# Other places in the step order for weight maxima, second-layer weight work, conversions and low parts, and another order of the last blocks' parts

## The chip, the cores and the metric

One core of one Trainium2 chip runs the kernel. The time is that of one execution on the device in microseconds; shorter is better. The kernel before takes 1488.77 us, the median of three runs between 1488.62 and 1488.83.

## The reference

Two parts follow one another: a gated linear attention over 4 batches, 8 heads, 768 positions and 48 columns a head, and a layer of 8 experts over the 3072 tokens that come out of it. The routing weights P are balanced in eight rounds, and every expert computes every token.

```python
f = 1.0 / (1.0 + np.exp(-f_logit))
for t in range(S):
    state = f[:, :, t, :, None] * state + np.einsum('bhd,bhe->bhde', k[:, :, t], v[:, :, t])
    y[:, :, t] = np.einsum('bhd,bhde->bhe', q[:, :, t], state)
...
logits = x @ w_gate                      # x: (3072, 384), 8 experts
P = np.exp(logits - logits.max())
for _ in range(8):
    P /= P.sum(1, keepdims=True) + 1e-09
    P /= P.sum(0, keepdims=True) + 1e-09
    P *= N / E
for e in range(E):
    h = np.maximum(x @ w1[e], 0.0)       # w1[e]: (384, 1024)
    out += P[:, e:e + 1] * (h @ w2[e])   # w2[e]: (1024, 384)
```

## The kernel before

Engine names are those of the profile: PE multiplies matrices, PEld loads its weights, DVE is the vector engine, ACT the scalar engine, POOL the general one, SP issues transfers.

**Numbers.** An fp32 operand of a product is split into two fp16 tensors, a high part (name with h: w1h, xh, hh, kh) written by ACT as a scaled copy, and a low part (w1l, xl, hl, kl) written by DVE or POOL as operand minus high part. A product is then three PE products: high by high, high by low, low by high.

**First part, up to about 491 us.** The attention runs in chunks (`early_item` for the first three items, `item` for the others; tiles q, kb, ql, vl, am, u, st, sl, aps, kvps, xl). As soon as a block of tokens has its output, experts 0 and 1 compute it in the plain way (`moe_tile`, `moe`): first layer into the bank hps, hh and hl from it, second layer into the bank yps, copied by ACT to yr and written to DRAM. These products fill PE between the attention's. The weights of the two experts come from `load`: SP starts the transfer into w1r or w2r, ACT makes w1h or w2h, DVE makes w1l or w2l, each at a step of its own. Which step is written out by hand: `FIRSTAT` and `SECONDAT` give, for each of the eight pieces of expert 0 and of expert 1, the steps at which its ACT and its DVE instruction are issued; `FILL` says how many products of the plain experts are put into a step. Instructions of an engine run in the order in which they are issued (`pin` chains them), so a step number is a place in every engine's queue. The Sinkhorn rounds and the conversion of the tokens for the second part (`convert`: sums xs by POOL, xah and xbh by ACT, xal and xbl by DVE, three maxima xmx a batch by DVE) follow, started at the steps `CONVSTEP` and `KSTEP`.

**Second part, from about 491 us.** Experts 2 to 7 are computed with fewer products. There are 48 periods (6 experts, 2 halves of the hidden columns, 4 batches; the table `ORDER`). A period multiplies tokens by first-layer weights as 3x3 blocks by 3x2 blocks in 15 block products (`PRODUCTS`); 15 linear forms of the tokens (xa, xb) and of the weights (k1h, k1l) go in, and the products are added up in the PSUM banks A to F. `SLOTS` gives the order of the 15 products with their banks; after each product comes what `EVENTS` lists for it: ACT copies a bank (cp), DVE adds a copy to a bank or starts bank E or F from bank D and a copy (init), ACT and DVE read the finished blocks (kh, kl, kah, kal, and the sums kr and kf), and ACT and DVE or POOL split the sums (kgh, kgl). Between the products of a period stand those of the second layer of the period before: three blocks (`paired`), each of which goes through eight parts with seven block products into the banks kyps and kxps, whose sums (part, xx, yy, acc) ACT, DVE and POOL form. A bank that is read has to be left before PE writes it again: this is how PE comes to wait for DVE and ACT.

Other work is given to a product's number by further tables: `W1AT` (`W1AT0` in period 0) for a piece of first-layer weights (`prepare_w1`: transfer k1r, sums k1s by POOL, a maximum wmx, k1h by ACT, k1l by DVE), `W2AT` (`W2AT0`, `W2AT1`, `W2AT3` in the first periods) for a piece of second-layer weights (`prepare_w2`: k2r, wmx, k2h, sums k2s, k2l), `READDAT` for the outputs of experts 0 and 1 that come back from DRAM (`readds`: yb, scaled by ACT to yz, added to acc by POOL), `MAXAT` for the maxima of the weights of experts 0 and 1 (`first_maxima`: a transfer k1rm or k2rm, then a maximum wmx), `CHECKAT` for other checks, `CONVAT` for the conversion of the last batch. The maxima feed a test at the end (`verdict`, tiles gd_t, gd_r, flag) of whether the fp16 scales suited the data.

After period 47 the blocks not yet finished are carried on by the string `ENDING`, one character a step: a dot issues the events of the next product number, a digit takes two parts of that block, v one step of the test. `ENDX` names the banks of these blocks.

Of the kernel before, what the change touches and what calls it, by code (L numbers as in the profile page):

```python
# [19 lines left out]
C = 64  # L20
# [4 lines left out]
KT = 3  # L25
# [62 lines left out]
ENDING = '.0.11.0.1..12.v12.22....vv32v3v34v3vvvvv4v34vv44'
# [188 lines left out]
def fast(ctx, tc, qkf, vbd, wg, w1, w2, out, flag):  # L277
# [83 lines left out]
    def load(e, k, j):  # L361
# [13 lines left out]
        ws[e][k - 1].append(pair)  # L375
# [13 lines left out]
    def moe(e, u, w):  # L389
# [5 lines left out]
        for f in range(FT):  # L395
# [4 lines left out]
            for a, x, k in [(wh, x, k) for k in range(KT) for x in (xh, xl)] + [(wl, xh, k) for k in range(KT)]:  # L400
                mm(out=ps, lhsT=a[:, k, fs], rhs=x[:, k, :], start=(n == 0), stop=(n == 8))
                n += 1
                if n < 9:
                    yield 1
# [1085 lines left out]
```

## Time and profile before

| | |
|---|---|
| median of three runs | 1488.77 us |
| the profiled execution's own time | 1490.45 us |
| its span, first to last instruction | 1488.7 us |
| mean granted clock of PE | 0.995 |
| busy: PE, PEld | 98%, 85% |
| busy: DVE, ACT, POOL | 86%, 70%, 70% |
| moved by DMA | 96.01 MB |
| PE's longest single wait (start, for DVE's ind) | 3.0 us |

A row of the timeline reads: start in the span, duration, engine, line, operation, result and operands, number of instructions, and in brackets the idle time ahead of it with the instruction that ended it. Names have no buffer numbers there, so that kb_A stands for bank A of every period. PE's products run one into the other: a product of 256 columns is shown with about 0.27 us and begins some 0.11 us after the one ahead of it, so a wait shorter than about 0.16 us does not appear in the brackets. A row of the stretches reads: from and to, length, and then the busy time of PE, PEld, DVE, ACT and POOL, each with its number of instructions, PE's granted clock (1.00 is full), the share of the DMA engines and GB/s.

### The profile page before, as it was taken

How to read it: one execution, taken by the hardware profiler on the slowest of the kernel's cores; microseconds unless marked ns; L12 is line 12 of the kernel's file. 1: busy time of each engine (PE TensorE's matmuls, PEld its weight loads, DVE VectorE, ACT ScalarE, POOL GpSimd, SP SyncE). 2: the span in 40 equal slices, each digit the busy share in tenths (PEclk: the TensorE clock that was granted, in tenths of full speed). 3: DMA queues.
4: the chain of work that ended last, by engine and by line, in shares of the span. 5: the costliest groups of instructions: out<-in, count | busy, mean ns of one | idle time of the engine just before them, and what ended most of it. 6: DMA issues, size and time to landing. Idle time of an engine off the chain costs nothing. (4 is left out here: it accounts for less than half of the span.)

```text
span 1488.7 us, 40252 instructions
## 1 busy us (share of the span) xinstructions
PE 1457.8 (98%) x16051; PEld 1266.0 (85%) x16051; DVE 1279.4 (86%) x2507; ACT 1035.6 (70%) x2310; POOL 1039.4 (70%) x1203
## 2 busy tenths in 40 slices
PE   7999999999999999999999999999999999999997
PEld 4788887666666789999999999999999999999996
DVE  8878988896677698999999999999999999888876
ACT  6655556554434777887887888888877777777764
POOL 2244444455427666899999998999988888888763
PEclk9999999999999999999999999999999999999999
DMA  9455645541000101221112111111110011000012
GB/s 276 122 134 135 142 118 130 142 103 50 22 33 29 52 12 29 61 61 55 47 57 65 56 56 44 52 55 55 49 33 28 28 34 33 12 13 23 2 54 78
DMA packets 82806, 96.01 MB, mean 64 GB/s; under 512 B 49872, under 2 KB 66384, under 8 KB 82608
## 3 DMA queue, kind: packets, MB, share of 16 engines
q1 hardware_dynamic: 82176, 92.75, 22.6%
q8 instruction: 127, 2.08, 0.6%
q14 instruction: 71, 0.58, 0.1%
q10 hardware_dynamic: 432, 0.59, 0.1%
HBM read 69.53 MB, written 14.16 MB: 56 GB/s over the span
## 5 line engine op out<-in xcount | busy, mean ns | idle before, releaser
L305 PEld LDWEIGHTS <-k1h 128*128 128x128 f16 x2880 | 270.4, 98 | 31.8 <-issue 7.2
L305 PE MATMUL kyps<-k2h,kgh 128*128 128x192 f16 x1152 | 283.6, 246 | 1.0 <-ACT part L1197 1.0
L305 PE MATMUL kyps<-k2l,kgh 128*128 128x192 f16 x1152 | 283.6, 246 | 0.0
L305 PE MATMUL kyps<-k2h,kgl 128*128 128x192 f16 x1152 | 283.6, 246 | 0.0
L305 PEld LDWEIGHTS <-kgh 128*128 128x128 f16 x2304 | 212.4, 98 | 7.9 <-issue 1.3
L1370 POOL TENSOR_TENSOR kgl<-kf,kgh 128x512 f16<-128x512 f32 x141 | 182.4, 1293 | 6.4 <-ACT kgh L1367 6.2
L1239 POOL TENSOR_TENSOR acc<-acc,yy 128x384 f32<-128x384 f32 x129 | 129.3, 1002 | 76.3 <-DVE yy L1200 76.2
L1370 POOL TENSOR_TENSOR kgl<-kr,kgh 128x512 f16<-128x512 f32 x141 | 172.2, 1221 | 11.2 <-ACT kgh L1367 11.2
L1200 DVE SCALAR_TENSOR_TENSOR yy<-kyps,pes,part 128x192 f32<-128x192 f32 x258 | 107.1, 415 | 73.0 <-PE kyps L305 68.1
L305 PEld LDWEIGHTS <-k1l 128*128 128x128 f16 x1440 | 141.0, 98 | 16.5
L305 PE MATMUL yps<-w2h,hl 128*128 128x384 f16 x384 | 125.9, 328 | 2.2 <-DVE hl L457 2.1
L305 PE MATMUL yps<-w2l,hh 128*128 128x384 f16 x384 | 125.9, 328 | 1.4 <-DVE w2l L377 1.4
L305 PE MATMUL yps<-w2h,hh 128*128 128x384 f16 x384 | 125.9, 328 | 0.0
L305 PEld LDWEIGHTS <-w1h 128*128 128x128 f16 x1344 | 97.2, 98 | 33.6 <-issue 2.6
L305 PEld LDWEIGHTS <-kh 128*128 128x128 f16 x1152 | 108.2, 98 | 8.9 <-issue 2.5
L305 PEld LDWEIGHTS <-kgl 128*128 128x128 f16 x1152 | 112.8, 98 | 0.2 <-issue 0.2
L305 PEld LDWEIGHTS <-hh 128*128 128x128 f16 x768 | 74.4, 98 | 45.1 <-issue 1.0
L305 PE MATMUL hps<-xl,w1h 128*128 128x128 f16 (+1 forms) x672 | 109.2, 257 | 1.3 <-DVE xl L666 0.6
L305 PE MATMUL hps<-xh,w1h 128*128 128x128 f16 (+1 forms) x672 | 109.0, 257 | 0.1
L1197 ACT ACTIVATE kyps<-kyps 128x192 f32<-128x192 f32 x144 | 46.2, 321 | 79.5 <-PE kyps L305 77.4
L1367 ACT ACTIVATE kgh<-kf 128x512 f16<-128x512 f32 x144 | 91.9, 639 | 0.6 <-DVE kf L1344 0.6
L1367 ACT ACTIVATE kgh<-kr 128x512 f16<-128x512 f32 x144 | 91.3, 634 | 0.2
(298 smaller groups left out, 5306.0 us busy)
## 6 DMA issues: line engine op xcount, KB each, us to landing
q<-in_qkf_dram SPq DMA_DIRECT2D x23, 672.0 KB, 5.0
vr<-in_vbd_dram SPq DMA_DIRECT2D x24, 384.0 KB, 3.9
k1r<-in_w_dram SPq DMA_DIRECT2D x24, 384.0 KB, 3.1
ys<-yr SPq DMA_DIRECT2D x48, 192.0 KB, 2.9
k2r<-in_w_dram SPq DMA_DIRECT2D x24, 384.0 KB, 3.1
yb<-ys SPq DMA_DIRECT2D x48, 192.0 KB, 2.8
out_dram<-acc SPq DMA_DIRECT2D x21, 192.0 KB, 1.9
w1r<-in_w_dram SPq DMA_DIRECT2D x8, 384.0 KB, 10.0
```

The source lines that it names most:

```text
L305: ins = (nc.tensor.transpose if transpose else nc.tensor.matmul)(**kw)
L1197: pin(nc.scalar.activation(out=out, in_=in_, func=AF.Copy, **kw))
L1200: pin(nc.vector.scalar_tensor_tensor(out=y, in0=ps, scalar=p, in1=z, op0=ALU.mult, op1=ALU.add))
L1239: pin(nc.gpsimd.tensor_tensor(out=y, in0=y, in1=z.rearrange("p s d -> p (s d)"), op=ALU.add))
L1367: pin(nc.scalar.activation(out=hs['g', t][0][i], in_=hs['f' if i else 'r', t], func=AF.Copy))
L1370: pin((nc.vector if tag == str(PERIODS - 1) else nc.gpsimd).tensor_tensor(out=hs['g', t][1][i], in0=hs['f' if i else 'r', t], in1=hs['g', ...
```

## The change

Both kernels have the same instructions; what differs is their order on each engine. The tables after the change, each with what stood there before:

```diff
 EVENTS: after product n the listed events
-          6: (('init', 'E', '-', 6, 'D'), ('copy', 'A', 0)), ...
-          9: (('gf', 'A', 0), ('copy', 'C', 7), ('gd', 0, 'P')),
+          5: (('init', 'E', '-', 6, 'D'),), 6: (('copy', 'A', 0),), ...
+          9: (('gd', 0, 'P'), ('gf', 'A', 0), ('copy', 'C', 7)),
...
-          21: ..., 23: (('gh', 2, 1),), 24: (('gl', 2, 1),), 26: (('gl', 2, 0),)}
+          21: ..., 23: (('gh', 2, 1),), 25: (('gl', 2, 1),), 26: (('gl', 2, 0),)}
-W2AT = (3, 22, 25, 25, 27, 29, 30, 34, 38)
+W2AT = (4, 22, 25, 25, 27, 29, 30, 35, 39)
-READDAT = (9, 13)
+READDAT = (9, 14)
-MAXAT = (1, 10)
+MAXAT = (0, 6)
-ENDX = ('x', 'k0', 'x', 'k0')
+ENDX = ('x', 'k1', 'k0', 'k0')
-ENDING = '.0.11.0.1..12.v12.22....vv32v3v34v3vvvvv4v34vv44'
+ENDING = '.0.101..1..21v..12.v22.v..3v233v434vvvvvv3v444vv'
-CONVSTEP = (25, 53, 71)
-KSTEP = 43
+CONVSTEP = (28, 55, 70)
+KSTEP = 39
...
 for the two plain experts and the attention:
-            for a, x, k in [(wh, x, k) for k in range(KT) for x in (xh, xl)] + [(wl, xh, k) for k in range(KT)]:
+            for a, x in ((wh, xh), (wl, xh), (wh, xl)):
+                for k in range(KT):
...
-                for m, (a, x) in enumerate(((0, vh), (0, vl), (1, vh))):
+                for m, (a, x) in enumerate(((0, vh), (1, vh), (0, vl))):
...
-            for m, (a, x) in enumerate(((kh, qh), (kh, ql), (kl, qh))):
+            for m, (a, x) in enumerate(((kh, qh), (kl, qh), (kh, ql))):
```

`FIRSTAT`, `SECONDAT`, `W1AT0`, `W2AT0`, `W2AT1`, `W2AT3` and `CONVAT` have other numbers too, mostly by one to three steps, in `CONVAT` by up to thirteen; `load` puts its pair at a fixed index instead of appending it; three entries are added to `FILL` and a name for the batches that POOL converts, with the values that applied before. In the lines of the second kernel all numbers are one or two higher.

What this moves on DVE is seen in three places. The first is at 52 to 58 us of the profile before: carry is the attention's state, w1l_2 and w1l_3 are weights of the second expert, xl the low part of the attention's output (in these rows names stand without the expert's number and with a buffer number at the end). Before:

```order
L377 SCALAR_TENSOR_TENSOR w1l_0_869<-w1r_0_496,w1h_0_868 128x768
L377 SCALAR_TENSOR_TENSOR w1l_1_872<-w1r_1_537,w1h_1_871 128x768
L588 TENSOR_TENSOR carry_1001<-kvps_1_974,st_831 112x384
L377 SCALAR_TENSOR_TENSOR w1l_2_895<-w1r_2_556,w1h_2_894 128x768
L377 SCALAR_TENSOR_TENSOR w1l_3_898<-w1r_3_578,w1h_3_897 128x768
L666 SCALAR_TENSOR_TENSOR xl_301<-yps_925,xh_300 96x3x128
L666 SCALAR_TENSOR_TENSOR xl_301<-yps_925,xh_300 32x128 x3
```

After:

```order
L378 SCALAR_TENSOR_TENSOR w1l_2_895<-w1r_2_556,w1h_2_894 128x768
L378 SCALAR_TENSOR_TENSOR w1l_0_869<-w1r_0_497,w1h_0_868 128x768
L378 SCALAR_TENSOR_TENSOR w1l_1_872<-w1r_1_538,w1h_1_871 128x768
L590 TENSOR_TENSOR carry_1002<-kvps_1_972,st_831 112x384
L668 SCALAR_TENSOR_TENSOR xl_301<-yps_923,xh_300 96x3x128
L668 SCALAR_TENSOR_TENSOR xl_301<-yps_923,xh_300 32x128 x3
L378 SCALAR_TENSOR_TENSOR w1l_3_995<-w1r_3_578,w1h_3_994 128x768
```

Of the two w1l between carry and xl, w1l_3 has gone behind xl and w1l_2 ahead of w1l_0 and carry.

The second place is at 64 to 71 us: wmx<-k2r is the maximum over a piece of second-layer weights of the second part, the two hl are the low parts for one tile of the second expert, ql and vl belong to the attention. Before:

```order
L377 SCALAR_TENSOR_TENSOR w2l_3_1105<-w2r_3_706,w2h_3_1104 128x768
L718 SCALAR_TENSOR_TENSOR vl_137<-vr_992,vh_131 128x768
L1063 TENSOR_REDUCE wmx<-k2r_0_8356 128x1
L457 SCALAR_TENSOR_TENSOR hl_0_0_0_1217<-hps_0_0_0_1178,hh_0_0_0_1216 128x512
L723 TENSOR_TENSOR ql_1164<-q_3_990,qh_1163 112x512
L457 SCALAR_TENSOR_TENSOR hl_0_0_1_1259<-hps_0_0_1_1220,hh_0_0_1_1258 128x512
L696 SCALAR_TENSOR_TENSOR r_1289<-ft_120,ind 112x512
```

After:

```order
L378 SCALAR_TENSOR_TENSOR w2l_3_1062<-w2r_3_706,w2h_3_1061 128x768
L720 SCALAR_TENSOR_TENSOR vl_137<-vr_990,vh_131 128x768
L459 SCALAR_TENSOR_TENSOR hl_0_0_0_1217<-hps_0_0_0_1178,hh_0_0_0_1216 128x512
L725 TENSOR_TENSOR ql_1164<-q_3_988,qh_1163 112x512
L1065 TENSOR_REDUCE wmx<-k2r_0_8356 128x1
L459 SCALAR_TENSOR_TENSOR hl_0_0_1_1259<-hps_0_0_1_1220,hh_0_0_1_1258 128x512
L698 SCALAR_TENSOR_TENSOR r_1289<-ft_120,ind 112x512
```

The maximum stood ahead of the first hl and stands now behind it and ql, still ahead of the second hl.

The third place is at 523 to 529 us, in period 1: k1l_2 is a piece of first-layer weights for later periods, kr, kf and kl read the banks B, D and F, kb_A is the addition to bank A, acc the output. Before:

```order
L1375 SCALAR_TENSOR_TENSOR kl_2_8524<-kb_D,kh_2_8523 128x512
L1055 SCALAR_TENSOR_TENSOR k1l_2_8685<-k1s_2_8552,k1h_2_8684 128x640
L1350 SCALAR_TENSOR_TENSOR kr_2_8873<-kb_F,kr_2_8873 128x256
L1344 SCALAR_TENSOR_TENSOR kr_2_8873<-kb_D,kr_2_8873 128x256
L1344 SCALAR_TENSOR_TENSOR kf_2_8906<-kb_D,kr_2_8873 128x256
L1344 SCALAR_TENSOR_TENSOR kf_2_8906<-kb_D,kf_2_8906 128x256
L1200 SCALAR_TENSOR_TENSOR acc_8630<-kyps_1_8736,pes,part_1_8738 128x192
L1206 TENSOR_SCALAR acc_8630<-kyps_1_8736,pes 128x192
L1055 SCALAR_TENSOR_TENSOR k1l_2_8685<-k1s_2_8552,k1h_2_8684 128x640
L1323 TENSOR_TENSOR kb_A<-kb_A,cp_13_8890 128x512
```

After:

```order
L1377 SCALAR_TENSOR_TENSOR kl_2_8524<-kb_D,kh_2_8523 128x512
L1352 SCALAR_TENSOR_TENSOR kr_2_8875<-kb_F,kr_2_8875 128x256
L1346 SCALAR_TENSOR_TENSOR kr_2_8875<-kb_D,kr_2_8875 128x256
L1346 SCALAR_TENSOR_TENSOR kf_2_8907<-kb_D,kr_2_8875 128x256
L1346 SCALAR_TENSOR_TENSOR kf_2_8907<-kb_D,kf_2_8907 128x256
L1202 SCALAR_TENSOR_TENSOR acc_8630<-kyps_1_8738,pes,part_1_8740 128x192
L1208 TENSOR_SCALAR acc_8630<-kyps_1_8738,pes 128x192
L1057 SCALAR_TENSOR_TENSOR k1l_2_8688<-k1s_2_8569,k1h_2_8687 128x640
L1325 TENSOR_TENSOR kb_A<-kb_A,cp_13_8891 128x512
```

The first k1l_2 has gone from ahead of the four kr and kf to behind the two acc; the second has left this stretch. Ahead of it, in period 1, the three xal and the first xbl of the last batch each stand one to nine instructions earlier, with their xah and xbh on ACT. In periods from 6 on, the maximum wmx of MAXAT's second number stands ahead of the addition to bank B instead of ahead of that to bank D, the start of bank E ahead of two accumulations, and on POOL the first early output yz is added ahead of one kgl instead of behind it. In the end, the twelve products of kyps_46_1 stand between two groups of kyps_46_2, and yy_1 and xx_1 of that block come ahead of the reading of block 2 on DVE and ahead of kyps_2, kh_1 and kah_2 on ACT.

More of the change, by code (lines that the diff above doesn't have):

```diff
@@ L101 @@
 LEADS = 23
-FILL = ((0, 11.7), (1, 10.3), (2, 0), (5, 2), (6, 0), (7, 6), (9, 0), (10, 6), (12, 5.3), (23, 8.7), (43, 8.1))
+FILL = ((0, 11.7), (1, 10.3), (2, 0), (3, 0), (5, 2), (6, 0), (7, 6), (8, 6), (9, 0), (10, 6), (12, 5.3), (23, 8.7), (31, 8.7), (43, 8.1))
 LEAD = 8
-FIRSTAT = ((0,), (5,), (0, 7), (0, 6), (3, 9), (5, 10))
-SECONDAT = ((16, 19), (16, 19), (17, 20), (17, 20), (20, 22), (21, 22), (22, 24), (23, 25))
-CONVSTEP = (25, 53, 71)
-KSTEP = 43
+FIRSTAT = ((0,), (4,), (0, 7), (0, 5), (1, 9), (5, 10))
+SECONDAT = ((16, 19), (16, 19), (17, 18), (19, 21), (20, 21), (20, 21), (24, 24), (22, 25))
+CONVSTEP = (28, 55, 70)
+KSTEP = 39
 PUTOFF = 17
+X_BY_POOL = (0, 1)
 EPRIO = 100
@@ L374, in load @@
         pair = [wh, None]
-        ws[e][k - 1].append(pair)
+        ws[e][k - 1][j] = pair
         yield
@@ L399, in moe @@
             n = 0
-            for a, x, k in [(wh, x, k) for k in range(KT) for x in (xh, xl)] + [(wl, xh, k) for k in range(KT)]:
[L401 to L404, printed above, removed]
+            for a, x in ((wh, xh), (wl, xh), (wh, xl)):
+                for k in range(KT):
+                    mm(out=ps, lhsT=a[:, k, fs], rhs=x[:, k, :], start=(n == 0), stop=(n == 8))
+                    n += 1
+                    if n < 9:
+                        yield 1
             th, tl = (hp.tile([128, 2, 256], F16, name=f"h{q}_{e}_{u}_{f}", tag=f"k{q}{f // 6}{f % 6 // 3}{f % 3}").rearrange("p c t -> p (c t)")[:, 0:HS] for q in "hl")
@@ L733, in item @@
         for n in range(NB):
-            for m, (a, x) in enumerate(((kh, qh), (kh, ql), (kl, qh))):
+            for m, (a, x) in enumerate(((kh, qh), (kl, qh), (kh, ql))):
                 mm(out=aps[:, n, :], lhsT=a[:, n, :], rhs=x[:, cs[n]], start=(m == 0), stop=(m == 2))
@@ L739, in item @@
             for p in range(NP):
-                for m, (a, x) in enumerate(((0, vh), (0, vl), (1, vh))):
+                for m, (a, x) in enumerate(((0, vh), (1, vh), (0, vl))):
                     o = (a * NB + CT * p + c) * R
@@ L870, in fast @@
     okm = cst.tile([128, 4], F32, name="okm")
-    ws = [([], []) for e in range(NE)]
+    ws = [([None] * 4, [None] * 4) for e in range(NE)]
     def raw_pairs(pairs):
@@ L969, in convert @@
     def convert(b, raw_left):
-        eng = nc.gpsimd if b < 2 else nc.vector
+        eng = nc.gpsimd if b in X_BY_POOL else nc.vector
         xh, xl = xt[b]
```

10 lines of the change are left out of this document (5 added, 5 removed), and 9 rows, old and new, of the table EVENTS.

## The prediction

> **What bounds the kernel now.** I read the page first, then the stretches by stage, then the timeline of each stretch in which the matrix engine (PE) is idle. Two lines of the page:
>
> ```profile
> span 1488.7 us, 40252 instructions
> PE 1457.8 (98%) x16051; PEld 1266.0 (85%) x16051; DVE 1279.4 (86%) x2507; ACT 1035.6 (70%) x2310; POOL 1039.4 (70%) x1203
> ```
>
> PE is busy 98% of the span. The change adds and removes no product, so all that it can win is PE's waiting and the time in which PE's clock is down: 1488.7 - 1457.8 = 30.9 us idle, plus what busy time hides. The next view has one row for each stretch: length, busy time of PE, PEld, DVE, ACT and POOL with their counts, PE's granted clock, then DMA.
>
> ```profile
> 491.00:529.50 38.50, 34.05 (x319) 29.16 (x318) 32.95 (x62) 31.62 (x67) 22.15 (x32) 1.00 0.12 37
> 529.50:533.00 3.50, 3.01 (x17) 2.38 (x16) 3.50 (x10) 3.25 (x6) 3.19 (x7) 0.51 0.00 0
> 600.00:1064.00 464.00, 461.07 (x4882) 433.20 (x4880) 427.99 (x859) 375.97 (x869) 424.32 (x498) 1.00 0.19 56
> 1064.00:1455.00 391.00, 390.91 (x4177) 371.06 (x4176) 339.91 (x706) 300.46 (x700) 316.95 (x367) 1.00 0.09 26
> 1455.00:1488.70 33.70, 24.29 (x272) 22.74 (x269) 22.63 (x59) 12.32 (x31) 12.21 (x15) 0.95 0.24 86
> ```
>
> The last quarter, 1064 to 1455, has 0.09 us of idle: no edit can win there. What can be won lies at the start, where the paired products begin (491 to 533, 4.45 us idle and a stretch at half clock), in the end, and in 600 to 1064. There the idle time is only 2.93 us, but a product takes 464/4882 = 0.0950 us against 391/4177 = 0.0936 later: 4882 x 0.00144 = 7.0 us over the stretch, in small waits at the start of every second period.
>
> **The second expert's weights ahead of xl, 50 to 57 us.** Rows of DVE and PE (start, duration, in brackets the idle time before and its releaser):
>
> ```profile
> 53.16 1.82 DVE L377 SCALAR_TENSOR_TENSOR w1l<-w1r,w1h 128x768 f16<-128x768 f32 x2
> 54.89 1.48 DVE L666 SCALAR_TENSOR_TENSOR xl<-yps,xh 96x384 f16<-96x384 f32 x4
> 55.79 1.36 PE L305 MATMUL hps<-xl,w1h 128*128 128x128 f16 x12 [0.41 <-DVE xl L666]
> 66.39 0.83 PE L305 MATMUL hps<-xl,w1h 128*128 128x128 f16 x12
> ```
>
> PE waits 0.41 us for the low part xl of the tokens, and its twelve products take 1.36 us instead of the 0.83 of the same group later, since each third waits for its piece of xl: 0.41 + 0.53 = 0.94 us. The change puts one of the two w1l in front of xl (1.82/2 = 0.91 us) behind it. The four pieces of xl then end at about 55.4 at the latest, one piece ahead of each third. The w1l put off is of the second expert, whose products, among them those at 66.39, come some 8 us later. Gain 0.9 us (bounds 0.5 and 1.1).
>
> **The maximum in front of hl, 64 to 72 us.**
>
> ```profile
> 58.63 0.69 DVE L457 SCALAR_TENSOR_TENSOR hl<-hps,hh 128x512 f16<-128x512 f32 x1 [0.40 <-ACT hh L454]
> 67.07 0.59 ACT L454 ACTIVATE hh<-hps 128x512 f16<-128x512 f32 x1
> 64.91 2.03 DVE L718 SCALAR_TENSOR_TENSOR vl<-vr,vh 128x768 f16<-128x768 f32 x1
> 68.13 0.95 DVE L1063 TENSOR_REDUCE wmx<-k2r 128x1 f32<-128x768 f32 x1 [1.19 <-DMA k2r<-in_w_dram]
> 69.00 0.68 DVE L457 SCALAR_TENSOR_TENSOR hl<-hps,hh 128x512 f16<-128x512 f32 x1
> 69.60 1.04 DVE L723 TENSOR_TENSOR ql<-q,qh 112x512 f16<-112x512 f32 x1
> 70.56 0.68 DVE L457 SCALAR_TENSOR_TENSOR hl<-hps,hh 128x512 f16<-128x512 f32 x1
> 69.74 0.34 PE L305 MATMUL yps<-w2h,hl 128*128 128x384 f16 x1 [1.52 <-DVE hl L457]
> 71.70 0.33 PE L305 MATMUL yps<-w2h,hl 128*128 128x384 f16 x1
> ```
>
> DVE stands 1.19 us waiting for weights that no product needs yet, then takes their maximum (0.95 us); the first hl queues behind it, and PE behind hl (1.52 us). In the change the maximum comes after hl and ql. But DVE is not 0.9 us earlier here: from 58.63 to the end of vl at 66.94 it has no idle time, so it keeps only the 0.40 us that it waited for hh. vl ends at 66.5. hh ended at 67.66 and can come up to 0.9 earlier with PE; ACT has other copies ahead of it, so I take half: hl runs from 67.2 to 67.9, and PE goes on at 68.0 instead of 69.74. Now the maximum stands in front of the second hl: ql to 68.9, maximum to 69.8, second hl to 70.45. PE wants it 71.70 - 69.74 = 1.96 us after the first, at 69.95, so a new wait of 0.5 us appears, and PE passes this point at 70.5 instead of 71.70. Both edits together: 1.2 us. Without the 0.40, with hh as before: hl to 68.35, ql to 69.4, maximum to 70.3, second hl to 71.0, that is 0.7 us. If the new wait does not come: 1.75. I take 1.2, range 0.7 to 1.75. Up to 491 us the same hidden tiles follow with the weights in place; I take it that the lead is kept, and that the three maxima over the tokens, moved in the Sinkhorn stretch, exchange one small wait for another: 0, bounds 0.3 to either side. In three loops the products of one accumulation change places (kl with qh ahead of kh with ql, and the like); they are the same products, each needed at most a few products sooner or later, and I count nothing.
>
> **The second period of paired products, 510 to 533 us.**
>
> ```profile
> 512.87 0.42 DVE L1356 SCALAR_TENSOR_TENSOR kal<-kb_A,kah 128x256 f16<-128x256 f32 x1 [0.58 <-ACT kr L1336]
> 524.13 1.73 DVE L1055 SCALAR_TENSOR_TENSOR k1l<-k1s,k1h 128x640 f16<-128x640 f32 x1
> 526.89 0.42 DVE L1344 SCALAR_TENSOR_TENSOR kf<-kb_D,kf 128x256 f32<-128x256 f32 x1
> 527.88 0.82 DVE L1055 SCALAR_TENSOR_TENSOR k1l<-k1s,k1h 128x640 f16<-128x640 f32 x1
> 528.61 0.69 DVE L1323 TENSOR_TENSOR kb_A<-kb_A,cp 128x512 f32<-128x512 f32 x1
> 527.37 0.28 PE L305 MATMUL kb_D<-xah,k1h 128*128 128x256 f16 x1 [1.05 <-DVE kf L1344]
> 529.99 0.37 PE L305 MATMUL kb_A<-xbh,k1h 128*128 128x256 f16 x1 [1.29 <-ACT cp L1321]
> ```
>
> PE waits 1.05 us until DVE has read bank D (kf), and 1.29 us more until DVE has added to bank A and ACT has copied it. DVE is full here; the k1l of 1.73 us is not urgent (weights of a later period). The change puts it behind kf, and takes one xal (768 columns, like the maximum of 0.95 above: an estimate of its length) into the hole of 0.58 at 512; an xbl of two thirds of that width comes forward against it. Counted on DVE up to kf: -1.73, -0.95, +0.6, so kf could end 2 us earlier; but ACT's copy kr, which it needs, stands behind the xbh that comes forward with xbl, about half a microsecond more, so I count 1.5: kf, which ended at 527.3, ends at 525.8, before PE wants it at 527.37 - 1.05 = 526.3. The first wait is gone and PE is 1.0 us early; behind kf there still stand two additions, a k1l (0.82 now) and the addition to bank A, which ends 1.3 us earlier than at 529.3. So kb_A starts at 528.7 instead of 529.99: gain 1.3, range 0 (if the moved xah and xbh delay ACT's copies by as much) to 2.
>
> With it goes the half clock. Rows of the stretches by 3.4 us:
>
> ```profile
> 505.60:509.03 3.43, 2.13 (x19) 1.57 (x17) 3.40 (x9) 2.82 (x6) 3.19 (x8) 1.00 0.21 78
> 526.10:529.50 3.40, 1.54 (x15) 1.11 (x13) 3.37 (x9) 1.30 (x4) 0.73 (x2) 1.00 0.01 2
> 24.38:27.79 3.41, 1.78 (x35) 1.50 (x36) 3.35 (x6) 3.41 (x7) 0.77 (x1) 1.00 1.02 305
> 27.79:34.61 6.82, 5.38 (x28) 3.10 (x28) 6.79 (x10) 1.90 (x4) 1.51 (x1) 0.50 1.05 248
> ```
>
> Both half-clock stretches follow 3.4 us in which PE was busy about half the time (1.54 and 1.78); after 2.13 of 3.43 the clock stayed at 1.00. With one wait of 1.2 instead of two, PE is busy some 2.2 us of the same stretch, so I expect full clock. The 17 products begun in 529.99 to 533.0 took 3.0 us; at 0.0950 to 0.10 each (the mean above, and more since most are of the wider kind) they take 1.6 to 1.7, so 1.3 us is won; bounds 0 and 1.3. The stretch at 27.79 stays: the wait ahead of it is for weights whose place in DVE's sum is unchanged.
> The Trainium skill, "TensorE: Matmul & The Clock Gate", Part 1, says that PE falls to half clock after an idle window of about 3.4 us, in windows that do not begin with the kernel. Length and ratio agree with these rows; an idle window does not, as PE was busy 45% of the one before. By that page no wait of this size matters, the half clock has another cause, and the sum is the first of the rivals.
>
> **Periods 6 to 28.** Here the small waits stand behind DVE, which in every second period also makes new weights:
>
> ```profile
> 658.36 0.42 DVE L1200 SCALAR_TENSOR_TENSOR yy<-kyps,pes,part 128x192 f32<-128x192 f32 x1 [1.21 <-PE kyps L305]
> 680.73 1.74 POOL L1370 TENSOR_TENSOR kgl<-kf,kgh 128x512 f16<-128x512 f32 x1
> 684.67 1.15 POOL L1370 TENSOR_TENSOR kgl<-kr,kgh 128x512 f16<-128x512 f32 x1
> 682.47 1.23 DVE L1055 SCALAR_TENSOR_TENSOR k1l<-k1r,k1h 128x256 f16<-128x256 f32 x1
> 531.73 0.68 DVE L1055 SCALAR_TENSOR_TENSOR k1l<-k1r,k1h 128x256 f16<-128x256 f32 x1
> ```
>
> The moved maximum of the early experts' weights (as large as the 0.95 above) now stands ahead of the addition to bank B in the period whose DVE afterwards waits 1.21 us for PE: that hole hides it; without the hole it would cost its excess over the slack. The initial value of bank E goes ahead of two accumulations, which changes no sum. POOL adds the early output yz ahead of kgl instead of behind it; kgl comes 1.0 us later, at a product that lies several products after it. The loads of the early weights and of yb move by one to four products with their steps on SP's queue, and land well ahead of either place. None of this shortens what DVE does between 678 and kl, so the waits stay: 0.
> What can change is who meets whom: k1l took 1.23 beside POOL's work and 0.68 alone, kgl 1.74 and 1.15. The Trainium skill, "SBUF — State Buffer", Who interferes with whom, says that a DVE instruction with two SBUF inputs and a POOL instruction that reads SBUF exclude each other, the later one waiting out the earlier. The rows agree in kind (0.55 more, not a sum of both). Bounds: most of the 7.0 us won, 5.5, or one such meeting more for each of some twelve pairs of periods, 12 x 0.55 = 6.6 lost. The nearest rows, those of the unchanged sum on DVE, give 0.
>
> **The end.**
>
> ```profile
> 1460.21 0.42 DVE L1200 SCALAR_TENSOR_TENSOR yy<-kyps,pes,part 128x192 f32<-128x192 f32 x1 [0.83 <-PE kyps L305]
> 1464.75 0.24 PE L305 MATMUL kyps<-k2h,kgh 128*128 128x192 f16 x1 [0.79 <-ACT part L1197]
> 1467.82 0.24 PE L305 MATMUL kyps<-k2h,kah 128*128 128x192 f16 x1 [0.44 <-ACT xx L1197]
> 1469.94 0.24 PE L305 MATMUL kyps<-k2h,kh 128*128 128x192 f16 x1 [0.86 <-DVE yy L1200]
> ```
>
> Twelve products now stand between two groups that share a bank, and yy and xx of the middle tile come earlier, so the waits at 1464.75 and 1467.82 shrink. But the wait at 1469.94 is for a yy behind everything that DVE does from 1460.21 on, without a hole; that list holds the same instructions in both orders. PE gets there earlier and waits longer. One guard reduction more stands ahead of the next kgl. I take +0.1, bounds -0.3 and +0.6.
>
> **Sum.** -1.2 - 1.3 - 1.3 + 0.1 = -3.7 us. The profiled execution took 1490.45 us for its span of 1488.70; the median of the plain runs is 1488.77, so I take the difference to that: 1488.77 - 3.7 = 1485.1. A measurement of this kernel can tell 0.2%, 3.0 us, from no change: faster means under 1485.8, slower over 1491.7. The forecast lies close to that edge; its own range, by the terms' usual misses, is 1483.8 to 1486.3.
>
> **Rivals.** (a) Half clock stays, by another cause or because the windows fall otherwise once PE leads by 1.2 us, or ACT's copies eat the second gain: -1.2 - 1.3 + 0.1 = -2.4, 1486.4. For it: only three windows show the limit. Against: 45 and 52% against 62%. Chance 0.23. (b) Nothing is kept: the lead of 1.2 is lost where hl or sl is late again before 330 us, and xah ahead of bank C's copy eats the period: about 1488.5; the change does not do what its order says. 0.08. (c) DVE gains the quarter microsecond that each even period lacks, and the small waits go: 3.7 + 5.5, 1479.6. For it: the small waits are short. Against: DVE has no hole from 678 to kl. 0.13. (d) Slower: POOL's kgl, now behind yz, meets DVE's k1l in every pair and kl, for which bank B waits, comes later by that: with 0.8 us a pair, 12 x 0.8 = 9.6, 1494.7; from 0.56 on it ends above 1491.7. Against: kgl met DVE already. 0.07. The forecast keeps 0.49.
>
> **Chances and range.** Faster: 0.13 of (c), three quarters of the forecast's 0.49, a little of (a): 0.54. Slower: 0.07. Same: 0.39. The range leaves out (d), about half of (c) and a part of (b): 1480.3 to 1488.8.
>
> **What would show it.** Right: the twelve xl products take 0.83 without a wait; hl starts near 67.3 and PE's wait before it falls from 1.52 to about 1; a wait of about 0.5 before the twelfth product after it; kb_D at 526 without a wait, full clock at 530; 0.0950 us a product from 600 to 1064 as before; the wait for yy in the end longer than before. Wrong: a clock of 0.5 after 529, a wait of over 0.5 at the addition to bank B or at kl in every even period, or 0.0936 us a product from 600 on.

## The result and the profile after

The changed kernel takes 1481.12 us (median of six runs, 1481.05 to 1481.34), the kernel before 1488.78 us in the six runs beside it (1488.60 to 1488.92): 7.66 us less, ratio 0.9949 with the interval 0.9936 to 0.9962. The forecast was 1485.1, 3.7 us less: the sign was right, half of the size was missing. The two lines of the page:

```profile
span 1479.4 us, 40139 instructions
PE 1452.1 (98%) x16051; PEld 1265.3 (86%) x16051; DVE 1262.8 (85%) x2507; ACT 1040.0 (70%) x2310; POOL 1041.5 (70%) x1203
```

DVE, which does the same instructions, is busy 16.6 us less (1279.4 before); 16.3 of them are k1l's, whose 96 instructions took 105.3 us before and take 89.0 now. Not all of that is time won: behind 1064, where PE waits for next to nothing, one k1l of 640 columns in each pair of periods takes 0.85 us in place of 1.61. The stretches, in the columns of the prediction; the third is shifted so that it holds about the periods that lay in 600 to 1064:

```profile
491.00:529.50 38.50, 35.29 (x335) 30.45 (x334) 34.91 (x69) 34.03 (x72) 22.30 (x30) 1.00 0.10 32
529.50:533.00 3.50, 3.50 (x39) 3.19 (x37) 3.50 (x9) 1.60 (x6) 3.19 (x7) 1.00 0.00 0
591.00:1054.00 463.00, 461.71 (x4931) 438.13 (x4930) 418.68 (x866) 379.74 (x878) 423.96 (x500) 1.00 0.19 56
1054.00:1445.00 391.00, 390.92 (x4176) 370.96 (x4174) 336.83 (x707) 304.53 (x700) 321.02 (x366) 1.00 0.08 26
1445.00:1479.40 34.40, 24.40 (x274) 23.01 (x271) 22.02 (x59) 12.67 (x32) 12.77 (x16) 0.94 0.24 84
```

The half clock at 529.5 is gone, and in the third row a product takes 463/4931 = 0.0939 us in place of 0.0950: 4931 x 0.0011 = 5.4 us in a stretch for which the forecast had 0. This is close to 0.0936, which the prediction named as a sign of being wrong. To see where the time went I took, in the traces of both kernels, the start of the same product (the first into bank E) in each of the 48 periods, and the difference after less before:

| place (us of before) | difference | forecast for the part |
|---|---|---|
| 497, period 0 | -1.26 | -1.2 |
| 511, end of period 0 | -1.53 | |
| 556, after period 1 | -4.25 | -1.3 for waits, -1.3 for the clock |
| 597, period 5 | -4.25 | |
| 699, 781, 863 | -5.74, -6.50, -7.50 | 0 |
| 1069, period 28 | -9.88 | 0 |
| last product | -9.72 | |
| end of the span | -9.30 | +0.1 |

From 597 to 1069 the lead grows by about 0.5 us in each pair of periods. The profiled execution of before, 1490.45 us, lay 1.7 us above its median; that of after, 1481.13, on it. So the two traces differ by 9.3 us and the medians by 7.66; run e4 below takes up that remainder.

**The start.** Rows of DVE, then of PE, in the kernel after:

```profile
53.65 1.48 DVE L668 SCALAR_TENSOR_TENSOR xl<-yps,xh 96x384 f16<-96x384 f32 x4
66.94 0.69 DVE L459 SCALAR_TENSOR_TENSOR hl<-hps,hh 128x512 f16<-128x512 f32 x1 [0.75 <-ACT hh L456]
67.55 1.44 DVE L725 TENSOR_TENSOR ql<-q,qh 112x512 f16<-112x512 f32 x1
68.91 0.94 DVE L1065 TENSOR_REDUCE wmx<-k2r 128x1 f32<-128x768 f32 x1
69.78 0.67 DVE L459 SCALAR_TENSOR_TENSOR hl<-hps,hh 128x512 f16<-128x512 f32 x1
55.05 0.85 PE L306 MATMUL hps<-xl,w1h 128*128 128x128 f16 x12
67.69 0.34 PE L306 MATMUL yps<-w2h,hl 128*128 128x384 f16 x1 [0.23 <-DVE hl L459]
70.51 0.34 PE L306 MATMUL yps<-w2h,hl 128*128 128x384 f16 x1 [0.69 <-DVE hl L459]
```

The twelve products of xl take 0.85 us without a wait (1.36 and 0.41 of wait before); the wait at the first hl falls from 1.52 to 0.23 (to about 1 was said), the foreseen wait at the second hl appears (0.69; 0.5 was said), and PE passes it at 70.51, forecast 70.5.

**Period 1.** DVE, then PE:

```profile
523.87 0.42 DVE L1346 SCALAR_TENSOR_TENSOR kf<-kb_D,kf 128x256 f32<-128x256 f32 x1
524.87 0.81 DVE L1057 SCALAR_TENSOR_TENSOR k1l<-k1s,k1h 128x640 f16<-128x640 f32 x1
524.90 0.27 PE L306 MATMUL kb_D<-xah,k1h 128*128 128x256 f16 x1
526.97 0.27 PE L306 MATMUL kb_A<-xbh,k1h 128*128 128x256 f16 x1 [0.75 <-ACT cp L1323]
```

kf is done before PE wants bank D, the wait of 1.05 is gone, and that for bank A is 0.75 in place of 1.29. The product into bank A, at 529.99 before, comes 529.99 - 526.97 = 3.02 us earlier; 1.53 of this was there at 511, so 1.49 are won here. Note k1l: 640 columns in 0.81 us here, in 1.73 before.

**Periods 6 to 28.** The pair of periods at 678 of after, DVE and then POOL:

```profile
677.23 0.55 DVE L1057 SCALAR_TENSOR_TENSOR k1l<-k1r,k1h 128x256 f16<-128x256 f32 x1
679.37 0.95 DVE L1057 SCALAR_TENSOR_TENSOR k1l<-k1r,k1h 128x384 f16<-128x384 f32 x1
676.50 1.00 POOL L1262 TENSOR_TENSOR acc<-acc,yz 128x384 f32<-128x384 f32 x1 [0.97 <-ACT yz L1261]
677.46 1.34 POOL L1372 TENSOR_TENSOR kgl<-kf,kgh 128x512 f16<-128x512 f32 x1
```

The k1l of 256 columns takes 0.55 us; before it took 1.23 at the same place. POOL, which now has the addition of yz ahead of kgl, stands idle 0.97 us for yz. This was the candidate for the missing 5 us, and the first thing to test.

**The end.** The waits of PE that are left there:

```profile
1454.64 0.24 PE L306 MATMUL kyps<-k2h,kh 128*128 128x192 f16 x1 [0.43 <-DVE yy L1202]
1460.32 0.24 PE L306 MATMUL kyps<-k2h,kh 128*128 128x192 f16 x1 [1.82 <-DVE yy L1202]
1468.10 0.24 PE L306 MATMUL kyps<-k2h,kgh 128*128 128x192 f16 x1 [0.24 <-ACT part L1199]
1471.35 0.24 PE L306 MATMUL kyps<-k2h,kh 128*128 128x192 f16 x1 [0.61 <-DVE acc L1202]
```

As said: the wait of 0.79 for part and that of 0.44 for xx are gone, and the one for yy behind DVE's list has grown from 0.86 to 1.82. A new wait of 0.43 for yy stands at 1454.64; the last two rows have their like before (0.23 at 1477.83 and 0.61 at 1481.07). In all PE waits 3.10 us here, 2.93 before.

### The profile page after: what moved, and what is told of

The parts are those of the page before. It is cut to its first block, busy times and chain, and to the rows that moved or that the text cites. A ratio compares the mean times of both kernels' runs of the same rounds, so it can differ in the third digit from the quotient of the medians.

```text
span 1479.4 us, 40139 instructions
## 1 busy us (share of the span) xinstructions
PE 1452.1 (98%) x16051; PEld 1265.3 (86%) x16051; DVE 1262.8 (85%) x2507; ACT 1040.0 (70%) x2310; POOL 1041.5 (70%) x1203
## 4 chain that ended last, share of the span: by engine, by line
PE 88%; DVE 7%; ACT 2%; issue 1%; POOL 1%; DMA 0%; DVEq 0%; ACTq 0%; POOLq 0%
PE kyps L306 28%; PE yps L306 13%; PE hps L306 10%; PE kb_A L306 8%; PE kb_B L306 8%; PE kb_D L306 6%; PE kxps L306 4%; PE kb_C L306 4%; PE kb_E L306 2%; PE kb_F L306 2%; PE kvps L306 1%; PE aps L306 1%; POOL kgl L1372 1%; DVE w1l L378 0%; DVE hl L459 0%
## 5 line engine op out<-in xcount | busy, mean ns | idle before, releaser
L1241 POOL TENSOR_TENSOR acc<-acc,yy 128x384 f32<-128x384 f32 x129 | 134.2, 1040 | 60.5 <-DVE yy L1202 60.5
L1323 ACT ACTIVATE cp<-kb_A 128x512 f32<-128x512 f32 x144 | 86.1, 598 | 3.2 <-PE kb_A L306 1.7
L306 PE MATMUL hps<-xh,w1l 128*128 128x128 f16 (+1 forms) x672 | 85.0, 257 | 0.0
```

Of the source, the lines that this page charges most:

```text
L306: ins = (nc.tensor.transpose if transpose else nc.tensor.matmul)(**kw)
L1241: pin(nc.gpsimd.tensor_tensor(out=y, in0=y, in1=z.rearrange("p s d -> p (s d)"), op=ALU.add))
L1323: pin(nc.scalar.activation(out=fresh(ev[2]), in_=bk, func=AF.Copy))
```

## The experiments

**Which edit made the 5 us.** One entry of EVENTS alone in the kernel before, and the same entry taken back in the kernel after:

```diff
 e1: the kernel before          e2: the kernel after
-24: (('gl', 2, 1),)           -25: (('gl', 2, 1),)
+25: (('gl', 2, 1),)           +24: (('gl', 2, 1),)
```

> The kernel before with one number of the change: kgl of block 2 from the sum kf one product later, so that on POOL the early output yz is added ahead of it in the 24 periods from 5 to 28; nothing moves on another engine. Theory A (in every second period POOL's kgl and its other work no longer run beside DVE's k1l, and DVE reaches kl early enough): the 0.5 us lost in each of eleven pairs of periods goes, about 5.5 us, 1483.2. Theory B (the maxima of the early experts' weights in front of bank D's addition held DVE up, and moving them gives the gain): no change, 1488.8. Theory C (the earlier start of bank E gives it): no change, 1488.8.

> The changed kernel with that one number as before, so that POOL again splits kf ahead of adding yz (and two instructions of DVE in the last block change places). Theory A: the waits at kl in every second period come back, about 5.5 us more than the changed kernel, 1486.6. Theories B and C: as the changed kernel, 1481.1.

e1: 1484.05 us (1482.69 to 1484.36), ratio 0.9964 (0.9951 to 0.9978). e2: 1486.16 us (1486.02 to 1486.30), ratio to before 0.9981 (0.9972 to 0.9990), 5.04 over the kernel after. Theory A holds both ways, and theory C falls with e1, where bank E starts as late as before. In e1 the order on PE, DVE and ACT is that of the kernel before, and POOL alone has 24 pairs of neighbours exchanged; in e2 two neighbours on DVE in the last block change places too. In e2 the rows of DVE and POOL at the same pair:

```profile
678.12 1.23 DVE L1057 SCALAR_TENSOR_TENSOR k1l<-k1r,k1h 128x256 f16<-128x256 f32 x1
680.94 0.95 DVE L1057 SCALAR_TENSOR_TENSOR k1l<-k1r,k1h 128x384 f16<-128x384 f32 x1
676.38 1.74 POOL L1372 TENSOR_TENSOR kgl<-kf,kgh 128x512 f16<-128x512 f32 x1
678.08 0.99 POOL L1262 TENSOR_TENSOR acc<-acc,yz 128x384 f32<-128x384 f32 x1
```

k1l is issued 0.04 us behind POOL's addition of yz and ends 0.28 us after it: it waited the rest of it out. In after it is issued 0.73 us behind the same instruction, and waits only 0.27.

**The moved maximum.**

```diff
-MAXAT = (0, 6)
+MAXAT = (1, 10)
```

> The changed kernel with the maxima of the early experts' weights at products 1 and 10 again, as before. Theory A: as the changed kernel, 1481.1, within 1 us. Theory B: the waits come back, 1486.6. Theory C: 1481.1.

1481.23 us (1481.11 to 1481.43): as the kernel after. The place of the maxima is worth nothing here, so theory B falls.

**The kernel before once more**, to see how its own executions differ; no edit.

> The kernel before once more, for a second profile. The changed kernel's span is 9.3 us shorter than that of the profiled execution before, while the medians differ by 7.66 us. Theory D (the half clock at 529.5 to 533 us is not met by every execution, since the windows of the gate do not begin with the kernel; it cost the profiled execution 1.3 to 1.7 us above the median): a span of about 1487.0 and full clock near 530 in most executions. Theory E (the half clock belongs to every execution of the kernel before, and the profiled one was longer elsewhere): half clock at 529 to 533 again.

1488.82 us (1488.56 to 1490.55, eight runs). Over all 77 runs of the kernel before made for this study there are two groups with nothing between them: 52 from 1488.41 to 1489.14 (median 1488.73) and 25 from 1489.97 to 1490.61 (median 1490.25), 1.52 us apart. The profiled execution of this run, 1489.97, is of the upper group, and its trace has the half clock:

```profile
529.50:533.00 3.50, 3.12 (x18) 2.42 (x18) 3.50 (x10) 3.15 (x6) 3.19 (x7) 0.53 0.00 0
```

e1 has the same two groups, 1482.69 and 1482.83 against 1484.05 to 1484.36, and half clock in its profile, of the upper one. The kernel after and e2, e3 have one group each. All three profiles that show the half clock (before, this one, e1) lie in the upper group. There is no trace of the lower one; that it lacks the half clock is inferred from the distance of 1.52 us, close to what the half clock takes by the prediction's count (1.3), and from the kernel after, whose profile has full clock and whose times form one group. The mean granted clock on record for each execution goes the same way: 0.9946 over the 25 of the upper group, 0.9969 over the 46 of the lower for which it was kept. One stretch of 3.4 us at half clock makes 0.0011 of it, so the upper group has this much and more, and the records don't say where. Read so, the half clock costs 1.5 us, which theory D had, in a third of the executions, and the median does not contain it.

**The start back.**

```diff
-FIRSTAT = ((0,), (4,), (0, 7), (0, 5), (1, 9), (5, 10))
-SECONDAT = ((16, 19), (16, 19), (17, 18), (19, 21), (20, 21), (20, 21), (24, 24), (22, 25))
+FIRSTAT = ((0,), (5,), (0, 7), (0, 6), (3, 9), (5, 10))
+SECONDAT = ((16, 19), (16, 19), (17, 20), (17, 20), (20, 22), (21, 22), (22, 24), (23, 25))
```

> The kernel after with FIRSTAT and SECONDAT as before, which brings the two w1l ahead of xl at 53 us and the maximum ahead of hl at 68 us back; all else as after. Theory A (the lead of 1.2 us won at 50 to 72 us is kept to the end): 1481.1 + 1.2 = 1482.3 us (1481.8 to 1482.9), and PE reaches the second part 1.2 us later than in the kernel after. Theory B (later waits swallow that lead): 1481.1 us.

1481.72 us (1481.58 to 1481.76): 0.60 more than after, between the two. In the trace PE is 1.18 us later at 496 and 1.13 up to 1038; there a small wait of the kernel after (0.22 us at 1054.7) does not occur, which leaves 0.84; after the last product the span is 0.3 us shorter, which is no more than the scatter there (see the run on the end). The lead is won as said and arrives by half.

**The k1l of period 1 back.**

```diff
-W1AT0 = (16, 17, 18, 19, 19, 23, 23, 27, 27, 32, 34, 35, 41)
+W1AT0 = (16, 16, 17, 19, 19, 23, 23, 27, 27, 31, 32, 34, 41)
```

> The kernel after with W1AT0 as before: in period 1 one k1l of 640 columns stands ahead of kr and kf again, four places on DVE and none on another engine. Theory A (this k1l makes the two waits of period 1, and these make the half clock in part of the executions): 1481.1 + 1.3 = 1482.4 us in executions with full clock and about 1.5 us more, 1483.9, in those with half clock at 529 to 533 us, so times in two groups 1.5 us apart. Theory B (the moved xal and the later conversions made the gain of period 1): 1481.1 us and one group of times.

1481.77 us (1481.68 to 1482.01), one group: 0.65 more. Both waits are back, the first of them small, and PE's busy share of the 3.4 us ahead of 529.5 is 2.11/3.40 = 62%:

```profile
525.15 0.28 PE L306 MATMUL kb_D<-xah,k1h 128*128 128x256 f16 x1 [0.26 <-DVE kf L1346]
527.76 0.27 PE L306 MATMUL kb_A<-xbh,k1h 128*128 128x256 f16 x1 [1.29 <-ACT cp L1323]
526.10:529.50 3.40, 2.11 (x23) 1.83 (x21) 3.40 (x9) 2.38 (x5) 2.71 (x6) 1.00 0.00 0
```

**yz behind the sums on POOL**, to tell "kgl must come after yz" from "k1l must not meet POOL":

```diff
-25: (('gl', 2, 1),)
-READDAT = (9, 14)
+24: (('gl', 2, 1),)
+READDAT = (10, 14)
```

> The kernel after with kgl of block 2 one product earlier again (as in the run that moved only this back, 1486.2 us), and with the early output yz one product later, so that on POOL a sum k2s of 0.57 us a piece, and no longer the addition of yz of 1.0 us, follows kgl when DVE comes to its k1l of 256 columns. Theory A (k1l waits out whichever POOL instruction has begun just before it): k1l takes about 0.85 us in place of 1.23 there and half or more of the loss goes, 1482.5 to 1484.5 us. Theory B (kgl itself stands too early on POOL, whatever follows it): 1486.2 us.

1486.20 us (1486.07 to 1486.40): the time that theory B gave. But the rows of DVE and POOL are those of theory A:

```profile
678.10 0.82 DVE L1057 SCALAR_TENSOR_TENSOR k1l<-k1r,k1h 128x256 f16<-128x256 f32 x1
680.50 1.36 DVE L1057 SCALAR_TENSOR_TENSOR k1l<-k1r,k1h 128x384 f16<-128x384 f32 x1
678.05 1.32 POOL L1075 TENSOR_TENSOR k2s<-k2r 128x192 f32<-128x192 f32 x2
680.29 1.16 POOL L1372 TENSOR_TENSOR kgl<-kr,kgh 128x512 f16<-128x512 f32 x1
```

The first k1l took the 0.82 that was said, and the second, which nobody had looked at, met the next kgl: 1.36 in place of 0.95. The sum of the two is 2.18 us as in e2. Neither theory as written stands: A's instruction behaved, its sum did not.

**The order of the end back.**

```diff
-ENDX = ('x', 'k1', 'k0', 'k0')
-ENDING = '.0.101..1..21v..12.v22.v..3v233v434vvvvvv3v444vv'
+ENDX = ('x', 'k0', 'x', 'k0')
+ENDING = '.0.11.0.1..12.v12.22....vv32v3v34v3vvvvv4v34vv44'
```

> The kernel after with ENDX and ENDING as before, so with the order of the last blocks' parts of the kernel before. Theory A (the waits of the end only change places, since the same list of DVE work from 1450 us on sets them): 1481.1 us, within 0.3. Theory B (the other order wins 0.5 us or more in the end that something else hides): 1481.6 us or more. Theory C (it costs 0.4 us or more, as the span's last 7 us are 0.4 longer in the kernel after): 1480.7 us or less.

1480.64 us (1480.61 to 1480.88), ratio to before 0.9944 (0.9930 to 0.9957): theory C. The new end costs about 0.5 us, and this kernel has the lowest times of the study. This rests on the times: its five runs all lie below the six of after, though the intervals of the two ratios overlap. The trace doesn't show the cause. Its last product comes 0.14 us earlier than in after, but 0.11 of these were there at 1443, ahead of the moved work; and the rest of the span behind the last product is 0.2 us shorter, while that rest goes from 6.78 to 7.20 us in the traces that share the new order. The mechanism stays open.

**yz later still**, so that the second k1l finds POOL idle:

```diff
-25: (('gl', 2, 1),)
-READDAT = (9, 14)
+24: (('gl', 2, 1),)
+READDAT = (12, 14)
```

> The kernel after with kgl of block 2 one product earlier again (1486.2 us alone) and the early output yz three products later, so that POOL does kgl, two k2s, the other kgl, waits there for yy, and adds yz after that. Theory A (each k1l of DVE waits out the POOL instruction that began just before it; what counts is the sum of the two k1l of a pair of periods, 2.18 us with 1486.2 us and 1.50 us with 1481.1 us): the k1l of 256 columns takes 0.82 us, that of 384 columns finds POOL idle and takes about 0.5, sum 1.3, and the loss goes: 1481.1 us (1480.6 to 1482.5). Theory B (kgl itself must stand behind the addition of yz): 1486.2 us.

1485.54 us (1484.64 to 1485.89). Again neither number, but the trace decides. Rows of DVE and POOL at the pair, then of ACT and PE elsewhere:

```profile
678.11 0.82 DVE L1057 SCALAR_TENSOR_TENSOR k1l<-k1r,k1h 128x256 f16<-128x256 f32 x1
680.51 0.55 DVE L1057 SCALAR_TENSOR_TENSOR k1l<-k1r,k1h 128x384 f16<-128x384 f32 x1
679.34 1.16 POOL L1372 TENSOR_TENSOR kgl<-kr,kgh 128x512 f16<-128x512 f32 x1
681.47 1.00 POOL L1241 TENSOR_TENSOR acc<-acc,yy 128x384 f32<-128x384 f32 x1 [0.97 <-DVE yy L1202]
622.54 0.61 ACT L1261 ACTIVATE yz<-yb,pes 128x384 f32<-128x384 f32 x1 [1.22 <-DMA yb<-ys]
625.00 0.27 PE L306 MATMUL kb_A<-xah,k1h 128*128 128x256 f16 x1 [0.69 <-ACT cp L1323]
```

The second k1l, issued as kgl ends, takes 0.55 us. Where e2 has two short waits in a pair (0.22 and 0.23 us ahead of products into bank B at 684.5 and bank A at 690.3), this trace has none, although kgl stands as early as in e2. What it has in their place is new: two products after the first yz its buffer yb has not yet landed again, ACT waits for it (14 times, 9.7 us in all), the bank copies stand behind, and PE waits for them. The times of the eight runs scatter more than those of the other kernels with one group; that the instant of landing differs between them is likely, but only one was traced.

**All of period 1 back.**

```diff
-W1AT0, CONVAT, CONVSTEP, KSTEP as in the kernel after
+W1AT0, CONVAT, CONVSTEP, KSTEP as in the kernel before
```

> The kernel after with W1AT0, CONVAT, CONVSTEP and KSTEP as before, so that k1l, xal, xbl and their copies stand in period 1 as in the kernel before; the start and POOL's order as after. Theory A (both waits of period 1 come back, PE is busy under 55% of the 3.4 us ahead of 529 us, and part of the executions goes to half clock): 1481.1 + 1.3 = 1482.4 us in some executions, 1483.9 in others, two groups 1.5 us apart. Theory B (the lead of 1.2 us from the start moves the windows, so no half clock): one group at 1482.4. Theory C (the half clock belongs to any order whose start is late): one group, 1481.1 to 1481.8.

1481.77 us; the five runs are 1481.62, 1481.71, 1481.77, 1482.09 and 1483.31. The last stands 1.5 us above the others, as the upper group of before does; the profiled execution was one of the others and has full clock, at a busy share of 62% in 526.1 to 529.5. So two groups, as A said, though the upper one is seen by its time alone and only once. The lower is at +0.65, not +1.3.

**The conversion alone back.**

```diff
-CONVAT = (0, 6, 6, 8, 11, 13, 14, 21, 23, 23, 34, 34, 37)
-CONVSTEP = (28, 55, 70)
-KSTEP = 39
+CONVAT = (3, 6, 6, 8, 11, 13, 14, 18, 21, 21, 24, 26, 27)
+CONVSTEP = (25, 53, 71)
+KSTEP = 43
```

> The kernel after with CONVAT, CONVSTEP and KSTEP as before, so the conversion of the last batch in period 1 as before but k1l behind kr and kf as after. The run with only W1AT0 back lost 0.65 us of the 1.3 us that both should be worth. Theory A (the two moves add up): 1481.1 + 0.65 = 1481.75 us (1481.5 to 1482.1). Theory B (either move alone is enough for the rest): 1481.1 us. Theory C (the conversion is the larger part): 1482.2 us or more.

1481.41 us (1481.22 to 1481.53), 0.29 more: between A and B, and hardly clear of the scatter, since the kernel before, lower group alone, has medians from 1488.63 to 1488.89 on the different occasions. In the traces the losses at 531 do add up: 0.95 us for e6, 0.27 for e11, 1.10 for both in e10. Afterwards they shrink at two places where the kernel after has a small wait that these lack: in e10 by 0.25 at 714 and by 0.28 at 1059.

**yz apart, with the old end**: the second yz moved into the next period so that yb has time to land (READDAT is counted on over the end of a period here).

```diff
-25: (('gl', 2, 1),)
-READDAT = (9, 14)
-            at_slots(n, READDAT, again)
+24: (('gl', 2, 1),)
+READDAT = (12, 22)
+            at_all(n, READDAT, again)
 ENDX, ENDING as in the kernel before
```

> As the run before with the early output yz late (kgl of block 2 one product earlier than in the kernel after), but the second yz of a period eight products later again, in the next period, so that its transfer has ten products of time in place of two; and the order of the end as in the kernel before, which alone gave 1480.6 us. Theory A (only the meetings of k1l with POOL's instructions made the loss of 5.0 us, and the 9.7 us that ACT waited for the transfers of yb made what was left of it in the run before): the two k1l of a pair take 1.4 us as in the run before, ACT's waits for yb are gone, and the time is 1480.6 us (1480.1 to 1481.5). Theory B (kgl stands too early on POOL in any case): 1485.7 us. Theory C (a yz ahead of kal or kr on POOL costs by itself): between the two, 1482 to 1484 us, with waits of PE behind kal or kr.

1486.39 us (1486.28 to 1486.51). A's 1480.6 is missed by 5.8 us, and the number is near B's. ACT's waits for yb are gone. DVE and POOL at the pair:

```profile
675.22 1.62 DVE L1057 SCALAR_TENSOR_TENSOR k1l<-k1s,k1h 128x640 f16<-128x640 f32 x1
677.74 1.08 DVE L1057 SCALAR_TENSOR_TENSOR k1l<-k1r,k1h 128x256 f16<-128x256 f32 x1
680.40 0.95 DVE L1057 SCALAR_TENSOR_TENSOR k1l<-k1r,k1h 128x384 f16<-128x384 f32 x1
675.16 1.00 POOL L1262 TENSOR_TENSOR acc<-acc,yz 128x384 f32<-128x384 f32 x1
676.11 1.31 POOL L1349 TENSOR_TENSOR kr<-kr 128x256 f32<-128x256 f32 x1
677.38 1.15 POOL L1372 TENSOR_TENSOR kgl<-kf,kgh 128x512 f16<-128x512 f32 x1
```

The second yz, with its data ready in advance, now stands ahead of kr and kgl, and POOL goes from one to the next without a hole: all three k1l meet it. I had reckoned with the first yz and with ACT, and not with where the second would fall on POOL. But kgl stands behind a yz in this kernel and the loss is there all the same, so B as worded falls with A's number.

What orders all these runs is the time of the last three k1l of a pair (640, 256 and 384 columns), read at 673 to 686 us of each trace; a fourth, of 640 columns, stands 3.5 us ahead of them and takes 1.30 to 1.38 us in all. The loss is PE's delay against the kernel after that a pair adds:

| kernel | k1l of the pair | sum | loss a pair | median |
|---|---|---|---|---|
| e9 | 1.35 + 0.82 + 0.55 | 2.72 | 0, and 3.9 in all behind yb | 1485.54 |
| after | 1.35 + 0.55 + 0.95 | 2.85 | 0 | 1481.12 |
| e1 | 1.35 + 0.55 + 0.95 | 2.85 | 0 | 1484.05 |
| before | 1.35 + 1.23 + 0.95 | 3.53 | 0.5 | 1488.78 |
| e2 | 1.35 + 1.23 + 0.95 | 3.53 | 0.53 | 1486.16 |
| e7 | 1.35 + 0.82 + 1.36 | 3.53 | 0.53 | 1486.20 |
| e12 | 1.62 + 1.08 + 0.95 | 3.65 | 0.53 | 1486.39 |

Up to 2.85 us DVE reaches kl and the addition to bank A in time; at 3.53 each pair loses half a microsecond. No run lies between the two.

## Why the prediction was right, and where it failed

**Start: right.** 1.26 us of lead against 1.2, with the wait at the second hl that was foreseen; the wait at the first fell further than said. That all of it is kept to the end was wrong: taking it back costs 0.60.

**Period 1: right in place, and in size by the trace.** Of the 4.25 - 1.53 = 2.72 us won from 511 to 556, 1.49 are there at the product into bank A (forecast 1.3), and 1.23 come in the half clock and just behind it (forecast 1.3). What arrives at the end is less: with the old order back and full clock (e10) 0.95 us are lost in this stretch of the trace and 0.65 in the median.

**Half clock: gone as said, but the sum was made against the wrong time.** The stretch is gone and was worth 1.2 us by the traces, 1.5 by the two groups (forecast 1.3). The step that failed is "so I take the difference to that": the profiled execution stood 1.68 us above the median, and this was, by the two groups, the half clock itself, which two thirds of the plain executions seem not to have. It should have counted 0 in the median.

The limit that the three windows gave, a busy share of about half, does not hold. In the trace of before the granted clock changes at 27.79, 34.61, 529.54 and 532.96 us, that is 2, 145 and 1 times 3.41 us apart, so the windows lie on a fixed grid; the same distances, whole multiples of 3.41 us, are in every trace. On that grid, in before, the 3.41 us from 24.38 were busy 1.78 (52%) and half clock followed, those from 20.97 were busy 1.71 (50%) and it did not; in after those from 1458.07 were busy 1.60 of 3.42 (47%) and it did not either. What does set it is open. The 62% of e6 and e10 from 526.1 to 529.5 belong to no window of theirs: there the grid falls at 523.8 and 527.2, the waits are shared out between two windows, 2.39 and 2.90 us busy in e6, 2.01 and 2.99 in e10, and the clock stays. The grid's place against the kernel differs between executions: the first drop to half clock comes at 27.79, 27.61 and 27.54 us in before, e4 and e1, and at 25.52 in e10, 2.27 us apart and so no whole window. That a third of the executions of before is in the upper group fits this, but with no trace of the lower group it is not shown.

The Trainium skill, "TensorE: Matmul & The Clock Gate", says that the window of about 3.4 us runs freely and does not start with the kernel; the grid of the traces and two groups of times of one kernel agree with that, since the same waits then fall into one window or into two. Its "idle" does not agree: PE was busy 45% of the time ahead.

**Periods 6 to 28: wrong, and this is the missing half.** The step that failed reads "None of this shortens what DVE does between 678 and kl, so the waits stay: 0". The edits shorten no instruction of DVE, but the entry that moves kgl on POOL shortens a wait inside one: k1l from 1.23 to 0.55 us. The lead grew by 9.88 - 4.25 = 5.63 us; e1 and e2 give that one entry 5 to 6 us. The prediction took 0.68 us for k1l "alone", but that row, at 531.73, stood beside POOL too: a sum k1s ran until 0.40 us after its start, and 0.40 + 0.28 = 0.68. Free of POOL, 0.55 us for 384 columns and 0.81 for 640 give 0.55 - 0.13 = 0.42 for 256, and the one such row, in e6 at 528.91, has 0.41. The right rows were at hand, yet I asked only whether POOL's kgl would meet k1l once more (rival d) and laid the gain with no mechanism on rival (c). (c) is what happened, at a chance of 0.13. Its 1479.6 was reckoned with the half clock (1.3) and a milder end. That 1481.12 lies in the stated range is owed to the half of (c) that the range took in, and is luck as far as the forecast's own terms go: they reached 1485.1 with 1.3 us that the median does not contain.
The Trainium skill, "SBUF — State Buffer", Who interferes with whom, says that the later of the two waits the earlier out. The rows agree with that to the hundredth: in e2, 0.95 us to the end of POOL's instruction and 0.28 behind it; in after, 0.27 and the same 0.28. POOL pays likewise where it comes second: kgl took 1.74 us at 680.73 of before, begun while a k1l ran, and 1.15 at 684.67. So what counts is the instant at which each is issued.

**End: too small.** Waits of PE changed places as described, from 2.93 to 3.10 us in all. The lead shrank by 0.16 us from 1069 to the last product, 0.13 of this in small waits from 1318 to 1443, ahead of the moved work; and the rest of the span grew by 0.42, as much as it scatters between traces with one order of the end (6.78 to 7.20 us with the new one). e8 gives the whole edit 0.48 us of loss where +0.1 was forecast, inside its bounds.

**The sum in the traces:** -1.26 - 0.27 (period 0, not looked into) - 1.49 - 1.23 - 5.63 + 0.16 + 0.42 = -9.3, the difference of the spans. Without the 1.5 us between the two groups, 7.8, beside 7.66 in the medians. **Open:** taken back one by one, start, POOL's entry, period 1 and end give 0.60 + 5.04 + 0.65 - 0.48 = 5.8 of 7.66 us. POOL's entry alone in the kernel before gives 1488.73 - 1482.76 = 6.0 in the lower groups, in the kernel after 5.0, and small waits that come and go at 714 and 1054 account for about 0.5 of what a part shows when it alone is taken back; the second-layer tables, the three loops and the other entries of EVENTS were not tried alone.

## What to carry to other kernels

Of a step that moves on POOL, look at every two-input DVE instruction issued while it runs, and at the next one too: lay both queues side by side in time, since the later one pays the rest of the earlier, and a hole of POOL at the right moment can be worth more than its work. Before a profile's time is compared with medians, see whether repeated runs fall into groups, and which group the profile is of. A lead won early is worth what the last small wait downstream leaves of it; measure it at the end and not where it is won.

## What the runs showed of the hardware that was not expected

- A DVE instruction can be doubled by POOL with no semaphore between them: k1l of 640 columns took 0.81 us where POOL was idle, 1.35 in most of the meetings shown here, and once 2.06 (after, 955.39, where it waited for two kgl one behind the other); that of 256 columns took 0.41 to 1.24. The trace shows it as busy time of DVE, not as a wait.
- One and the same kernel has two groups of times, 52 and 25 of 77 executions, 1.52 us apart, with the half clock near 529 us in both of its profiles, which are of the upper group.
- Half clock cost nothing in a stretch where PE isn't the bound. From 20 to 40 us, where DVE is busy 97%, after has a granted clock of 0.83 and e3, which has the same order up to 610 us, of 0.74; yet PE is at the same product in e3 at 495.6 us, 0.1 us sooner than in after:

```profile
20.00:40.00 20.00, 15.05 (x196) 10.84 (x194) 19.38 (x30) 12.74 (x24) 3.44 (x4) 0.83 0.84 253
```

```profile
20.00:40.00 20.00, 15.99 (x191) 11.81 (x189) 19.39 (x30) 12.70 (x24) 3.43 (x4) 0.74 0.94 263
```
